# The silu MLP's up products as two pairs of token groups with seven products each: groups 2 and 1 at 512 tokens, groups 3 and 4 as twice 384

## The chip, the cores and the metric

The kernel runs on one core of one Trainium2 chip, as one program. The metric is device time in microseconds (us), median of repeated executions. Beside it there is one profiled execution, read here as rows of its trace: every instruction of the engines TensorE (PE), VectorE (DVE), ScalarE (ACT), GpSimd (POOL) and SyncE (SP), with what each waited for.

## The reference

The inputs are fp32; three layers follow one another:

```python
scores = where(mask, q @ k.T / 8, -1e9)          # 4 batches, 8 heads, 576 positions, head width 64
x = softmax(scores) @ v                          # masks: last 32 positions (heads 0-3), every 32nd (heads 4-7)
x = x.transpose(0, 2, 1, 3).reshape(2304, 512)   # 2304 tokens
x = ((x @ w_a) * (x @ w_b)) @ w_out              # gated MLP, 512 -> 1536 -> 512
h = x @ w_in2                                    # silu MLP, 512 -> 2048
out = (h * sigmoid(h)) @ w_out2                  # 2048 -> 512
```

## The kernel before

**Products.** Every fp32 operand is split into a high and a low part (type fp32r), and each product is three passes: high by high, high by low, low by high (`PASSES`). The 2304 tokens are five groups: 0 to 3 of 512 tokens, group 4 of 256. A hidden piece is 128 hidden units. An "up" product of one piece for one group is 4 blocks of 128 inputs by 3 passes, 12 matmuls whose moving side is as wide as the group: 128x512, or 128x256 for group 4. The down products of the silu MLP have 128 tokens on the output's partitions and 512 outputs as the moving side, so they are 128x512 whatever the group; one hidden piece and 128 tokens are 3 matmuls.

**Direct part.** Up to some 453 us the loop over `PHASES` works through groups 0 and 1 of the gated MLP ("A"), then of the silu MLP ("B"), in blocks of 12 matmuls (`BLOCK`, 2.72 us by the planner). The attention of batches 1 to 3 runs between these products, its units placed by `PLAN` at numbered blocks until `ATT_END`. The weights come packed and are converted there; converted ones are also written to DRAM and read back by the second part.

**Late part.** All after that is a list of events with planned times (`at`, `products`), sorted and issued once (`run_events`); the planner counts 0.2267 us for a 128x512 matmul (`MM`) and 0.12 us for a 128x256 one (`MM_HALF`). It does not measure; on the chip an engine that comes late makes the others wait.

**A pair of groups.** Groups 2 and 3 are taken together: 2x2 blocks of weights by 2x2 blocks of (half of the inputs) by (group) need seven block products in place of eight (Strassen and Winograd). A `Chain` makes these seven for one block of hidden pieces; a `twin` runs two chains in turn, `CHAIN_ORDER` giving the order: 14 steps of 6 matmuls each. After some steps DVE and ACT combine the sums: ACT copies a sum out of PSUM (`u` or `p`), DVE adds the other (L1105), and for the silu MLP ACT takes a tanh (`th`), DVE makes `g` (L1133), ACT casts its high part and DVE subtracts the low part (L806), which gives `h` for the down products of the near group. The far group's `x` rows are kept in SBUF, and its down products run after all twins. DVE and ACT also split the weights (`w`, L1381 and L1380), among them sums of weight blocks `T` (L1390). The near group's down products (L1151, "fillers", 3 matmuls each) are put between the steps by the argument `places`; they are those of the quadrants that this twin and the one before it have finished.

**Order before.** Direct A0, A1, B0, B1; pair (2,3) of the gated MLP, twins then far down (453 to 633 us); group 4's gated MLP (633 to 687); pair (2,3) of the silu MLP, four twins and near down (687 to 805), far down (805 to 849); group 4's silu MLP, 16 pieces up at 128x256 and down (849 to the end).

Of the kernel before, what the change touches and what calls it, by code (L numbers as in the profile page):

```python
# [9 lines left out]
F32 = mybir.dt.float32  # L10
# [7 lines left out]
ALU = mybir.AluOpType  # L18
# [51 lines left out]
PHASES = [("A", 0), ("A", 1), ("B", 0), ("B", 1)]  # L70

HOMES = {"x": (0, 1), "y": (0, 3)}

OPERANDS = ("A11", "A12", "S1", "S2", "S3", "S4", "A22")  # L80
# [9 lines left out]
MM, MM_HALF, BLOCK = 0.2267, 0.12, 2.72  # L90
LEAD_RAW, LEAD_SUM, LEAD_SPLIT = 22.0, 9.0, 6.0

ATT_END = 115
# [8 lines left out]
    2: (37, [41, 49, 58, 66], 78),  # L102
    3: (78, [82, 89, 97, 105], 0),
# [15 lines left out]
def attention_gated_mlp_silu_mlp(  # L119
# [96 lines left out]

    def two(t, n=CC):

        return t.rearrange("p k t -> p (k t)").rearrange("p (s c t) -> p s c t", s=2, c=n)
# [10 lines left out]
    def x_tile(g):  # L230
        if g == NG - 1 and g not in x_t:
            both["s"] = t = home(1)
            x_t[g] = two(t[:, :4])
        if g not in x_t:
            x_t[g] = xpool.tile([P, 2, CC, G], F32R, tag="x%d" % HOMES["x"][g], name="x")
        return x_t[g]
# [482 lines left out]
    def place(c):  # L719
        if c >= STAY:  # L720
            return rpool.tile([P, DM], F32, tag="raw", name="raw")
        if c < CC:
            return pair_home()[:, CC + c]
        if "w" not in both:
            both["w"] = home(3, F32)
        return both["w"][:, c - CC]
# [162 lines left out]
    with tc.manual_schedule():  # L889
# [107 lines left out]
        sp, hs, ops, late = {}, {}, {}, {}  # L997
# [21 lines left out]
        def open_late():  # L1019
            att_ctx.close()  # L1020
            late["pool"] = pool = ctx.enter_context(
                tc.tile_pool(name="late", bufs=1, side="right", reuse_waits="tile")
            )
            t = pool.tile([P, 16, G], F32R, name="operands")
            for m, name in enumerate(("S2", "S1", "A22", "S4")):
                ops[name] = two(t[:, 4 * m:4 * m + 4], 2)
# [4 lines left out]

        def part(name, c, src):
            o = ops[name]
            nc.scalar.copy(out=o[:, 0, c], in_=src())
            nc.vector.tensor_tensor(out=o[:, 1, c], in0=src(), in1=o[:, 0, c].bitcast(F32), op=ALU.subtract)

        def put(key, c, tag, a, b, op):
            sums[key, c] = t = temp(*tag)
            nc.vector.tensor_tensor(out=t, in0=a(), in1=b(), op=op)

        sums = {}

        def operands(r2, r3, t0, step0, t1, step1):

            row = lambda r, c: lambda: r()[:, c]
            got = lambda key, c: lambda: sums[key, c]
            for m, (name, c) in enumerate([(n, c) for n in ("A11", "A12") for c in range(2)]):
                at(t0 + m * step0, part, name, c, row(r2, c + 2 * (name == "A12")))
            work = []
            for c in range(2):  # L1050
                work += [(put, "s1", c, ("p1", c), row(r3, c), row(r3, 2 + c), ALU.add)]
                work += [(put, "s2", c, ("u2", c), got("s1", c), row(r2, c), ALU.subtract)]
                work += [(part, "S2", c, got("s2", c))]
            work += [(part, "S1", c, got("s1", c)) for c in range(2)]
            for c in range(2):
                work += [(put, "s3", c, ("u3", 0), row(r2, c), row(r3, c), ALU.subtract)]
                work += [(part, "S3", c, got("s3", c))]
            work += [(part, "A22", c, row(r3, 2 + c)) for c in range(2)]
            for c in range(2):
                work += [(put, "s4", c, ("u3", 1), row(r2, 2 + c), got("s2", c), ALU.subtract)]  # L1060
                work += [(part, "S4", c, got("s4", c))]
            for m, (f, *a) in enumerate(work):
                at(t1 + m * step1, f, *a)

        def store_row(k):

            n = 2 * (k // 8)
            if n not in late:
                late[n] = home(n or 3, F32)
            return late[n][:, k % 8]  # L1070


        class Chain:
            def __init__(self, n, kind, j, c):
                self.n, self.kind, self.j, self.c = n, kind, j, c
                self.acc, self.q = {}, {}
# [5 lines left out]
            def multiply(self, s):  # L1082
                operand, piece, part, acc, begin = CHAIN[s]
                if begin:
                    self.acc[acc] = ring_tile() if acc == "X" else att_tile(False)
                w, x = sp[self.key(s)], ops[operand]
# [12 lines left out]
            def copied(self, name):  # L1099
                t = temp(name, self.c)  # L1100
# [23 lines left out]
        def gated(chains, quad, row):  # L1124
            out = tpool.tile([P, G], F32, tag="h32", name="h32") if row is None else store_row(row)
# [3 lines left out]
        def silu(chain, quad, row):  # L1129
            th = tpool.tile([P, G], F32, tag="a", name="th")  # L1130
            nc.scalar.activation(out=th, in_=chain.q[quad], func=AF.Tanh, scale=0.5)
            out = tpool.tile([P, G], F32, tag="h32", name="g2") if row is None else store_row(row)
# [11 lines left out]
        def down(accs, w, h, kind, d, first, last):  # L1144

            for wi, xi in PASSES:
                if kind == "o":
                    lhsT, rhs = sp[w][:, wi, d * P:(d + 1) * P], hs[h][:, xi]
                else:
                    lhsT, rhs = hs[h][:, xi, d * P:(d + 1) * P], sp[w][:, wi]  # L1150
                nc.tensor.matmul(  # L1151
                    accs[d], lhsT=lhsT, rhs=rhs, start=(first and wi == 0 and xi == 0), stop=(last and wi == 1)
                )

        def twin(n, kinds, js, half_n, fillers, places):
# [413 lines left out]
```

## Time and profile before

| what | value |
| --- | --- |
| median of 3 runs | 900.23 us (899.98 to 900.32) |
| span of the profiled execution | 897.1 us |
| PE busy | 885.1 us (99%) |
| DVE busy | 621.9 us (69%) |
| ACT busy | 538.0 us (60%) |
| POOL busy | 158.8 us (18%) |

The span runs from the first to the last instruction of the profiled execution. That execution's own time is the span and some 3 us around it, the median of the runs less the span. "Busy" adds up what an engine worked; a queue of matmuls counts as busy while the next waits for nothing.

### The profile page before, as it was taken

The numbers are of one execution on the slowest core, as the hardware profiler recorded it, in microseconds if no ns is written. First come the engines' busy times: TensorE is split into PE (matmuls) and PEld (weight loads), VectorE is DVE, ScalarE is ACT, GpSimd is POOL, SyncE is SP. The second block draws the span as 40 slices with busy tenths as digits, with TensorE's granted clock in tenths as the row PEclk, the third lists the DMA queues.
The fourth block names the chain that finished last, engine by engine and source line by source line (L and its number), as shares of the span: only waits on it lengthen the run. The fifth ranks groups of instructions, "written<-read, shape, count | busy, mean of one in ns | idle before, by whom it ended". The sixth has DMA issues, their size and how long they took to land.

```text
span 897.1 us, 16230 instructions
## 1 busy us (share of the span) xinstructions
PE 885.1 (99%) x5907; PEld 733.4 (82%) x5914; DVE 621.9 (69%) x1123; ACT 538.0 (60%) x1270; POOL 158.8 (18%) x230
## 2 busy tenths in 40 slices
PE   8899999999999999999999999999999999999998
PEld 5578788888888888888888888888999888888897
DVE  4587977758667775767777676765687766775475
ACT  4668898666876765555544434354675555554464
POOL 4545564343432310100000000000000000000000
PEclk9799999999999999999999999999999999999999
DMA  8999899798898982332322212133553221234461
GB/s 175 205 249 294 265 269 311 212 276 247 260 327 259 261 240 95 118 118 94 95 94 71 65 54 71 54 111 99 160 175 110 71 83 51 78 95 164 138 188 40
DMA packets 161584, 142.17 MB, mean 158 GB/s; under 512 B 96656, under 2 KB 119760, under 8 KB 161504
## 3 DMA queue, kind: packets, MB, share of 16 engines
q1 hardware_dynamic: 152166, 117.09, 46.5%
q0 software_dynamic: 7392, 23.23, 7.0%
q10 hardware_dynamic: 1946, 0.81, 0.5%
q8 instruction: 46, 0.75, 0.3%
q14 instruction: 34, 0.28, 0.1%
HBM read 118.55 MB, written 22.54 MB: 157 GB/s over the span
## 4 chain that ended last, share of the span: by engine, by line
PE 88%; DVE 3%; DMA 3%; ACT 2%; SPq 2%; issue 1%; POOL 0%; DVEq 0%; ACTq 0%; POOLq 0%
PE ring L795 24%; PE ring L1090 12%; PE acc L1507 10%; PE att L1090 9%; PE acc L1151 9%; PE acc L1485 6%; PE acc L1277 4%; PE ring L1151 4%; PE att L1151 4%; PE acc L795 3%; DMA words<-in_moe_w_a_dram 1%; PE att L470 1%; PE att L621 1%; PE att L572 1%; SPq L355 1%
## 5 line engine op out<-in xcount | busy, mean ns | idle before, releaser
L795 PE MATMUL ring<-x,w 128*128 128x512 f32 (+1 forms) x816 | 163.0, 354 | 0.4 <-DVE w L788 0.4
L795 PEld LDWEIGHTS ring<-x,w 128*128 128x128 f32 x816 | 133.4, 189 | 21.5 <-DVE w L788 1.0
L1381 DVE TENSOR_TENSOR w<-raw,w 128x512 fp32r<-128x512 f32 (+1 forms) x164 | 106.2, 655 | 28.0 <-ACT w L1380 25.1
L1380 ACT CAST w<-raw 128x512 fp32r<-128x512 f32 (+1 forms) x164 | 95.7, 592 | 19.6 <-PE att L1151 11.0
L795 PE MATMUL ring<-y,w 128*128 128x512 f32 x384 | 93.1, 392 | 0.0
L1507 PE MATMUL acc<-w,h 128*128 128x512 f32 x384 | 92.4, 391 | 0.0
L788 DVE TENSOR_TENSOR w<-raw,w 128x512 fp32r<-128x512 f32 x112 | 83.9, 757 | 9.3 <-ACT w L787 9.0
L1196 POOL DMA_DIRECT2D out_dram<-o x16 | 8.7, 546 | 458.7 <-DVE o L1195 456.2
L1507 PEld LDWEIGHTS acc<-w,h 128*128 128x128 f32 x384 | 71.6, 188 | 15.0
L795 PEld LDWEIGHTS ring<-y,w 128*128 128x128 f32 x384 | 71.5, 188 | 14.9
L805 ACT CAST h<-h 128x512 fp32r<-128x512 f32 (+1 forms) x48 | 27.2, 566 | 77.3 <-DVE h L1126 40.6
L1485 PE MATMUL acc<-h,w 128*128 128x512 f32 x288 | 70.4, 394 | 0.3 <-DVE h L806 0.2
L787 ACT CAST w<-raw 128x512 fp32r<-128x512 f32 x112 | 68.0, 621 | 0.2 <-DVE raw L765 0.2
L1485 PEld LDWEIGHTS acc<-h,w 128*128 128x128 f32 x288 | 53.3, 188 | 12.1 <-DVE h L806 0.5
L806 DVE TENSOR_TENSOR h<-g,h 128x512 fp32r<-128x512 f32 (+1 forms) x64 | 40.5, 632 | 28.9 <-ACT h L805 28.9
L1090 PE MATMUL ring<-operands,w 128*128 128x512 f32 x240 | 58.8, 389 | 0.0
L1090 PE MATMUL att<-operands,w 128*128 128x512 f32 x240 | 58.8, 389 | 0.0
L1090 PE MATMUL ring<-x,w 128*128 128x512 f32 x240 | 58.7, 389 | 0.0
L805 ACT CAST h<-g 128x512 fp32r<-128x512 f32 (+1 forms) x64 | 36.3, 567 | 35.8 <-DVE g L1477 29.1
L740 POOL TENSOR_SCALAR raw<-words 128x512 f16<-128x512 uint8 x56 | 52.1, 931 | 30.9 <-DMA words<-in_moe_w_in_dram 9.9
L1090 PEld LDWEIGHTS att<-operands,w 128*128 128x128 f32 x240 | 45.0, 188 | 9.4
L1090 PEld LDWEIGHTS ring<-operands,w 128*128 128x128 f32 x240 | 45.0, 188 | 9.4
(211 smaller groups left out, 1615.3 us busy)
## 6 DMA issues: line engine op xcount, KB each, us to landing
raw<-keptp SPq DMA_DIRECT2D x80, 256.0 KB
raw<-kepti SPq DMA_DIRECT2D x64, 256.0 KB
words<-in_moe_w_out_dram SPq DMA_DIRECT2D x28, 512.0 KB
raw<-kepto SPq DMA_DIRECT2D x45, 256.0 KB
words<-in_moe_w_in_dram SPq DMA_DIRECT2D x16, 512.0 KB
raw<-keptb SPq DMA_DIRECT2D x32, 256.0 KB
raw<-kepta SPq DMA_DIRECT2D x31, 256.0 KB
words<-in_moe_w_a_dram SPq DMA_DIRECT2D x12, 512.0 KB
```

The costliest lines, as they stand in the source:

```text
L740: nc.gpsimd.tensor_scalar(out=halves_of(made[c], F16, 1), in0=bytes_of(words[c], 8, 7), scalar1=-TINY, scalar2=127.5 * TINY, op0=ALU.mult, ...
L787: nc.scalar.copy(out=o[:, 0], in_=t)
L788: nc.vector.tensor_tensor(out=o[:, 1], in0=t, in1=o[:, 0].bitcast(F32), op=ALU.subtract)
L795: nc.tensor.matmul(ps[:, :T], lhsT=w[:, wi, c * P:(c + 1) * P], rhs=x[:, xi, c, :T], start=(c == 0 and wi == 0 and xi == 0), stop=(c == CC ...
L805: nc.scalar.copy(out=o[:, 0, :T], in_=t32[:, :T])
L806: nc.vector.tensor_tensor(out=o[:, 1, :T], in0=t32[:, :T], in1=o[:, 0, :T].bitcast(F32), op=ALU.subtract)
L1090: nc.tensor.matmul(self.acc[acc], lhsT=w[:, wi, (2 * part + c) * P:(2 * part + c + 1) * P], rhs=x[:, xi, c], start=(begin and c == 0 and m ...
L1151: nc.tensor.matmul(accs[d], lhsT=lhsT, rhs=rhs, start=(first and wi == 0 and xi == 0), stop=(last and wi == 1))
L1380: nc.scalar.copy(out=o[:, 0, cols], in_=t)
L1381: nc.vector.tensor_tensor(out=o[:, 1, cols], in0=t, in1=o[:, 0, cols].bitcast(F32), op=ALU.subtract)
L1485: nc.tensor.matmul(accs[d], lhsT=w[:, wi, d * P:(d + 1) * P], rhs=h[:, xi], start=(j == 0 and wi == 0 and xi == 0), stop=(j == N1 - 1 and ...
L1507: nc.tensor.matmul(accs[t][:, :DM], lhsT=h[:, xi, t * P:(t + 1) * P], rhs=w[:, wi, :], start=(j == 0 and wi == 0 and xi == 0), stop=(j == ...
```

## The change

`PHASES` loses B1. The late part begins with group 4's gated MLP, then takes pair (2,3) of the gated MLP as before. The silu MLP then has two objects `Pair("B", ...)`: groups 2 (near) and 1 (far) at 512 tokens, and groups 3 and 4 together, 768 tokens, as a near and a far half of 384 (`T34`), whose twins' matmuls are 128x384. Their down products stay 128x512, three blocks of 128 tokens for each half. Operand buffers get named slots, and `prepare` sets the operand work's planned times. `ATT_END` and `PLAN` put the attention of batches 2 and 3 into fewer blocks. In the diff's core:

```diff
-PHASES = [("A", 0), ("A", 1), ("B", 0), ("B", 1)]
+PHASES = [("A", 0), ("A", 1), ("B", 0)]
-MM, MM_HALF, BLOCK = 0.2267, 0.12, 2.72
+MM, MM_HALF, MM_SHORT, BLOCK = 0.2267, 0.12, 0.1733, 2.72
-ATT_END = 115
+ATT_END = 103
-    2: (37, [41, 49, 58, 66], 78),
-    3: (78, [82, 89, 97, 105], 0),
+    2: (37, [40, 47, 55, 62], 70),
+    3: (70, [73, 80, 88, 95], 0),
+        class Pair:
+            def __init__(self, mlp, near, far, T, rows):
+                self.mlp, self.near, self.far, self.T, self.rows = mlp, near, far, T, rows
+                self.mm = MM if T == G else MM_SHORT
...
-                    end = products(lambda s=s, chain=chain: chain.multiply(s), 6, MM, [chain.key(s)])
+                    end = products(lambda s=s, chain=chain: chain.multiply(s), 6, pair.mm, [chain.key(s)])
...
+        def fill(pair, g, j, accs):
+            return [fill_one(pair, g, j, d, accs) for d in range(CC if pair.mlp == "A" else pair.T // P)]
...
+        def second(pair, t_near, t_far, last):
+            near, far = {}, {}
+            down_p = lambda f: [x for j in (f, f + 1) for x in fill(pair, pair.near, j, near)]
+            for f in range(0, H2, 2):
+                n = ("p", f, pair.near)
+                if f:
+                    twin(pair, n, "ii", (f, f + 1), H2, down_p(f - 2 + H2) + down_p(f), dict.fromkeys(range(1 + (f == H2 - 2), 15), 1))
+                else:
+                    twin(pair, n, "ii", (f, f + 1), H2, down_p(f), dict.fromkeys(range(9, 15), 1))
+            for filler in down_p(H2 - 2 + H2):
                 products(*filler)
+            results(t_near, near, pair.T // P, nc.gpsimd, "vvvv")
...
+        t_down = second(pair12, groups[2][0], groups[1][0], False)
+        T34 = (groups[4][0] + T4 - groups[3][0]) // 2
+        pair34 = Pair("B", 5, 6, T34, (lambda c: y34()[:, c, :T34], lambda c: y34()[:, c, T34:]))
...
+        second(pair34, groups[3][0], groups[3][0] + T34, True)
```

**Order on TensorE, second to third twin of the pair that it concerns.** Before, in pair (2,3) of the silu MLP: L1090 are the steps of 6 matmuls, L1151 the fillers; the last step of the first chain is the first row, and the last row is the first filler that uses what this step finished.

```order
L1090 MATMUL att<-operands,w 128x512 x6
L1151 MATMUL acc_8085<-w,h 128x512 x3
L1090 MATMUL att<-operands,w 128x512 x6
L1151 MATMUL acc_8108<-w,h 128x512 x3
L1151 MATMUL acc_8124<-w,h 128x512 x3
L1151 MATMUL acc_8137<-w,h 128x512 x3
L1090 MATMUL ring<-x,w 128x512 x6
L1151 MATMUL acc_8085<-w,h 128x512 x3
```

Between the step and that filler stand two steps and four fillers. The same place in the changed kernel, in the pair of halves of 384 tokens (L1129 the steps, L1192 the fillers; `x1a` and `L_8354` are operand slots):

```order
L1129 MATMUL ring<-x3b,w 128x384 x6
L1192 MATMUL acc_8867<-w,h 128x512 x3
L1129 MATMUL ring<-x3b,w 128x384 x6
L1192 MATMUL acc_8884<-w,h 128x512 x3
L1129 MATMUL att<-x1a,w 128x384 x12
L1129 MATMUL ring<-L_8354,w 128x384 x6
L1192 MATMUL acc_8851<-w,h 128x512 x3
```

The two last steps of the twin (`x1a`, x12) now follow each other without a filler, and after the first of them only one step of it and one of the next twin (`L_8354`) stand ahead of the filler that uses its result. A twin there has 12 fillers in place of 16.

**Order on VectorE at the same place.** Before (`u` is the sum that the first chain's last step completes; the two rows of L1133 ahead of it make far rows):

```order
L1133 SCALAR_TENSOR_TENSOR x<-th,ring 128x512 x2
L1381 TENSOR_TENSOR w<-raw,w 128x512 x2
L1105 TENSOR_TENSOR u_8036<-u_8036,att 128x512
L1133 SCALAR_TENSOR_TENSOR g_8156<-th,u_8036 128x512
L806 TENSOR_TENSOR h<-g_8156,h 128x512
```

Behind the far rows there are two weight splits, then the sum. In the changed kernel:

```order
L1174 SCALAR_TENSOR_TENSOR x<-th,ring 128x384
L1416 TENSOR_TENSOR w<-raw,w 128x512 x2
L1174 SCALAR_TENSOR_TENSOR x<-th,ring 128x384
L1425 TENSOR_TENSOR T<-raw 128x256
L1425 TENSOR_TENSOR T<-raw,T 128x256
L1425 TENSOR_TENSOR T<-raw 128x256
L1425 TENSOR_TENSOR T<-raw,T 128x256
L1144 TENSOR_TENSOR u_9040<-u_9040,att 128x384
L1174 SCALAR_TENSOR_TENSOR g_9179<-th,u_9040 128x384
L829 TENSOR_TENSOR h<-g_9179,h 128x384
```

Four sums of weight blocks now stand between the second far row and the sum that leads to `h`.

## Rows read from the trace of the kernel before

**Rows 1.** The page, part 1: busy time of each engine

```profile
PE 885.1 (99%) x5907; PEld 733.4 (82%) x5914; DVE 621.9 (69%) x1123; ACT 538.0 (60%) x1270; POOL 158.8 (18%) x230
```

**Rows 2.** Busy time by stretch; columns as the first line names them

```profile
core 0: us, PE busy (x) PEld busy (x) DVE busy (x) ACT busy (x) POOL busy (x), PEclk, DMA share, GB/s
...
145.00:265.50 120.50, 120.50 (x964) 98.55 (x964) 82.32 (x141) 86.42 (x222) 47.13 (x69) 1.00 0.90 268
265.50:330.00 64.50, 64.50 (x516) 52.78 (x515) 46.59 (x78) 46.04 (x110) 17.64 (x24) 1.00 0.95 272
330.00:453.40 123.40, 123.40 (x784) 101.41 (x783) 85.91 (x149) 68.00 (x167) 8.12 (x11) 1.00 0.32 100
...
687.40:804.60 117.20, 117.20 (x519) 96.80 (x518) 84.97 (x150) 65.43 (x124) 0.00 (x0) 1.00 0.22 70
```

**Rows 3.** PE in time, its longest wait (start, us, work, idle before)

```profile
40.52 2.47 PE L795 MATMUL acc<-x,w 128*128 128x512 f32 x6 [2.62 <-DVE x L654]
```

**Rows 4.** PE in time, two stretches: 128x512 steps, 128x256 blocks

```profile
755.53 1.52 PE L1090 MATMUL ring<-x,w 128*128 128x512 f32 x6
756.89 0.84 PE L1151 MATMUL acc<-w,h 128*128 128x512 f32 x3
...
640.13 3.04 PE L795 MATMUL ring<-x,w 128*128 128x256 f32 x24
643.01 1.60 PE L1277 MATMUL acc<-h,w 128*128 128x256 f32 x12
```

**Rows 5.** Groups by shape from 633 us on (busy us, mean ns | idle before)

```profile
L806 DVE TENSOR_TENSOR h<-g,h 128x512 fp32r<-128x512 f32 x16 | 11.1, 691 | 6.5 <-ACT h L805 6.5
L806 DVE TENSOR_TENSOR h<-g,h 128x256 fp32r<-128x256 f32 x16 | 6.7, 420 | 0.5 <-ACT h L805 0.5
...
L1131 ACT ACTIVATE th<-u 128x512 f32<-128x512 f32 x16 | 10.1, 632 | 19.2 <-DVE u L1105 19.2
L1261 ACT ACTIVATE th<-acc 128x256 f32<-128x256 f32 x16 | 6.2, 385 | 12.1 <-PE acc L795 12.1
```

**Rows 6.** PE from the second twin to the third

```profile
733.10 0.84 PE L1151 MATMUL acc<-w,h 128*128 128x512 f32 x3
...
735.13 0.84 PE L1151 MATMUL acc<-w,h 128*128 128x512 f32 x3
...
740.58 0.84 PE L1151 MATMUL acc<-w,h 128*128 128x512 f32 x3
```

**Rows 7.** DVE in the second twin and on to the third

```profile
727.79 0.69 DVE L1105 TENSOR_TENSOR u<-u,att 128x512 f32<-128x512 f32 x1 [1.86 <-ACT u L1101]
...
733.92 0.69 DVE L1133 SCALAR_TENSOR_TENSOR x<-th,ring 128x512 f32<-128x512 f32 x1 [0.19 <-ACT th L1131]
734.53 1.29 DVE L1381 TENSOR_TENSOR w<-raw,w 128x512 fp32r<-128x512 f32 x2
735.74 0.68 DVE L1105 TENSOR_TENSOR u<-u,att 128x512 f32<-128x512 f32 x1
737.17 0.69 DVE L1133 SCALAR_TENSOR_TENSOR g<-th,u 128x512 f32<-128x512 f32 x1 [0.76 <-ACT th L1131]
738.55 0.69 DVE L806 TENSOR_TENSOR h<-g,h 128x512 fp32r<-128x512 f32 x1 [0.69 <-ACT h L805]
```

**Rows 8.** ACT after the product that ends at 756.89 us

```profile
757.09 0.59 ACT L1101 COPY u<-ring 128x512 f32<-128x512 f32 x1 [2.05 <-PE ring L1090]
```

**Rows 9.** DVE and PE in the second twin: sums T, first activation, first use

```profile
715.90 0.42 DVE L1390 TENSOR_TENSOR T<-raw,T 128x256 f32<-128x256 f32 x1
716.24 0.42 DVE L1390 TENSOR_TENSOR T<-raw 128x256 f32<-128x256 f32 x1
...
722.21 0.69 DVE L806 TENSOR_TENSOR h<-g,h 128x512 fp32r<-128x512 f32 x1
...
722.89 0.84 PE L1151 MATMUL acc<-w,h 128*128 128x512 f32 x3
```

**Rows 10.** The stretch behind PE's longest wait; columns as in rows 2

```profile
41.00:44.40 3.40, 3.40 (x32) 2.39 (x32) 1.10 (x2) 0.54 (x5) 0.78 (x1) 0.50 1.05 173
```

More of the change, by code (lines that the diff above doesn't have):

```diff
@@ L1043, in operands @@
[L1043 to L1063, printed above, removed]
@@ L1170, in twin @@
                         else:
-                            key = (chain.kind, 2, j)
+                            key = (chain.kind, pair.near, j)
                             at(end, keep_act, key, f, *a, None)
@@ L1245, in start4 @@
         def start4(kind, j):
[L1246 to L1247 removed]
+            ps = st4[kind] = ring_tile()
+            up4(kind, j, ps, x_tile(4))
         def copy4():
@@ L1308, in attention_gated_mlp_silu_mlp @@
                 for d in range(CC):
-                    down_one("o", "b", j, d, N1)
-        y3 = lambda: late[0]
-        operands(y2, y3, t_o3 + 6.0, 6.0, t_a4 + 3.0, (clock[0] - t_a4 - 8.0) / 18)
-        accp2 = {}
-        down_p = lambda f: [x for j in (f, f + 1) for x in fill("p", "i", 2, j, j == 0, j == N2 - 1, accp2)]
+                    products(*down_of(j, d))
+        pair = Pair("A", 2, 3, G, (lambda c: x_pair(2)[:, c], lambda c: x_pair(3)[:, c]))
+        pair.prepare(FIRST_OPERANDS, t_open - 22, 4.0)
@@ L1320, in attention_gated_mlp_silu_mlp @@
             else:
-                last_o = [down_of("o", "b", N1 - 1, d, N1) for d in range(CC)]
-                twin(("p", f), "ii", (f, f + 1), H2, last_o + down_p(f), {2: CC, **dict.fromkeys(range(9, 15), 1)})
-        for filler in down_p(H2 - 2 + H2):
+                twin(pair, ("o", f), "ab", (f, f), H1, [down_of(N1 - 1, d) for d in range(CC)], {2: CC})
+        for filler in down_o(H1 - 1):
             products(*filler)
-        results(2, accp2, CC, nc.gpsimd, "vvvv")
-        accp3 = {}
@@ L1341, in attention_gated_mlp_silu_mlp, with save_y, y2 @@
-        down_one("p", "i", N2 - 2, 0, N2)
-        for d in range(T4 // P):
-            for j in ((N2 - 1,), (N2 - 2, N2 - 1))[d]:
-                down_one("p", "i", j, d, N2)
-        for t in range(T4 // P):
-            at(clock[0], lambda t=t: result(groups[4][0], t, acc4["p", t], (epool, tpool)[t], "ea"[t], "va"[t], nc.sync))
+        def save_y(accs, out):
+            for d in range(CC):
+                nc.scalar.copy(out=out()[:, d, :G], in_=accs[d])
+        def y2():
+            if "y2" not in late:
+                late["y2"] = slot("L0", F32)
+            return late["y2"]
@@ new lines, in far_down @@
+        def far_down(pair, act, n, accs, tail=0):
+            for j in range(n):
+                key = (act, pair.far, j)
+                ready[key] = clock[0] - LEAD_SPLIT
+                at(clock[0] - LEAD_SPLIT - 0.1, keep_act, key, pair.row, j)
+                if j < n - tail:
+                    for filler in fill(pair, pair.far, j, accs):
+                        products(*filler)
+        pair12 = Pair("B", 2, 1, G, (lambda c: y2()[:, c], lambda c: ys[1][:, c]))
+        s1 = lambda: tpool.tile([P, G], F32, tag="a", name="s1")
```

284 lines of the change are left out of this document (151 added, 133 removed).

## The prediction

> **What bounds the kernel now.** I read the busy times first: PE works 885.1 of 897.1 us, DVE 621.9, ACT 538.0 [rows 1]. A share over the whole span hides stages, so next the busy time by stretch: in each stretch from 145 to 453 us and in the silu pair's twins (687 to 805 us) PE's busy time is the whole stretch [rows 2]. Then PE's waits in order of length: the longest is 2.62 us at 40.52 us [rows 3], at the start of the kernel, and the late part has none that counts. So the time is the sum of what PE issues, at the pace of its matmuls, and a change is worth the matmuls that it removes, less the waits that it creates where other engines no longer keep up. How near the others are is the last view: in the silu pair's twins DVE is busy 84.97 of 117.20 us [rows 2], but most of its idle time is waiting on ACT inside chains (0.7 us each time, [rows 7]); only one wait per twin, 1.86 us, is real slack [rows 7].
>
> **What the change removes and adds on PE.** Counted in the order of instructions: 128x512 matmuls fall from 3288 to 3096 (192 fewer), 128x256 from 624 to 432 (192 fewer), and 336 of 128x384 come. The silu MLP explains it: one direct group (384 matmuls of 512) becomes the far group of a pair, and 192 up matmuls of 256 for group 4 are merged into seven-product chains of 384. The price of one: six steps of 512 take 756.89 - 755.53 = 1.36 us, 0.2267 each; 24 of 256 take 643.01 - 640.13 = 2.88 us, 0.120 each [rows 4]. A 384-wide one does not occur before. Its bounds are these two, 0.120 and 0.2267; halfway in width, I take halfway in time, 0.1733. The sum: -192 x 0.2267 = -43.5, -192 x 0.120 = -23.0, +336 x 0.1733 = +58.2; together **-8.3 us**. At the two bounds the last term would be 40.3 or 76.2, so the saving could be 26 us or a loss of 10; two points on a line make me give the price 2% either way, 1.2 us.
>
> [...]
>
> **What is moved at no cost.** Group 4's gated MLP goes to the front of the late part, pair (2,3) of the gated MLP behind it: the same matmuls. Pair (2,1) of the silu MLP is pair (2,3)'s pattern with other tokens. The operand splits for the last pair lie in the far down of pair (2,1), 43.5 us of PE; I count some 34 us of DVE there, and without that cover they would cost their own length. The last results leave on SP, and the store behind the last matmul is one block of 128 tokens as before.
>
> **The waits it creates.** They sit in the four twins of the last pair. A step takes 6 x 0.1733 = 1.04 us, a filler 3 x 0.2267 = 0.68. With 12 fillers in place of 16 a twin takes 84 x 0.1733 + 36 x 0.2267 = 22.7 us on PE; one at 512 takes 132 x 0.2267 = 29.9.
>
> *DVE's price.* At 512 an operation of DVE takes 0.691 us, at 256 0.420; of ACT 0.632 and 0.385 [rows 5]. At 384 I take halfway again: 0.555 and 0.51. [...] Issued one behind the other, DVE's operations follow at shorter distances: 0.34 at 256 (715.90 to 716.24, [rows 9]), 0.605 at 512 (two splits, 734.53 to 735.74, [rows 7]), so 0.47 at 384. A twin of the last pair has 38 DVE rows that matter: 10 of 512, 10 of 256, 18 of 384, that is 6.05 + 3.4 + 8.5 = 18 us of issue, and its dozen waits on ACT are some 6 us more (each about 0.5 to 0.6 at 384, against 0.7 at 512). That is 24 us against PE's 22.7: **in these twins DVE is late by about 1.3 us a twin** where it now has 1.9 to spare.
>
> *The chain to an activation.* From the end of the step that completes a sum to the first operation on it: 757.09 - 756.89 = 0.2 us [rows 4, 8]. From the sum to `g` 737.17 - 735.74 = 1.43, from `g` to `h` 1.38, `h` 0.69 [rows 7]. Taking off 0.135 for each DVE operation and 0.12 for each ACT operation gives 1.18 + 1.12 + 0.55 = 2.85 at 384, so 3.05 us with DVE free. Before, PE has 740.58 - 735.13 = 5.45 us between that step and the filler that needs `h` [rows 6], and `h` was done at 739.24 [rows 7].
>
> *Second to third twin.* Now one step of this twin and one of the next stand there: 2 x 1.04 = 2.08 us. Even with DVE free PE waits 3.05 - 2.08 = 1.0. But four sums `T` stand ahead of `u`. Before, the second far row started 733.92 - 733.10 = 0.82 us behind its product [rows 6, 7]; that product now ends 1.72 us (a filler and a step) before our step's end E. So the far row starts at about E - 0.95, and 0.47 and four times 0.34 later `u` may start: E + 0.9. `h` is there at E + 3.7: a wait of 1.65. With DVE 0.8 us late (two thirds of a twin's lag) 2.45. I take **2.5**.
>
> *First to second twin.* A filler, two steps, a filler: 3.44 us, enough for 3.05: 0. *Third to fourth.* Three steps, 3.12 us; DVE free 0, with one us of lag **1.0**. *Behind the fourth.* A step and a filler, 1.72 us: at least 1.35, with lag **1.7**; then the second chain's `h`, 2.85 behind the first against three fillers, 2.04: **0.75**. *First activation of the second twin.* It has no margin at 512 already: `h` ends at 722.90, the filler starts at 722.89 [rows 9]. Now PE passes there with steps a quarter shorter, and the chain shrinks by a fifth only while it carries the same splits of 512: **1.4**. Small ones of the same kind in the other twins: **0.5**. Together **7.9 us**; with DVE free 3.75; with the lag carried over fully from twin to twin some 11.
>
> **The sum.** -8.3 + 7.9 = -0.4 on a span of 897.1, so 896.7; the median of the runs stands 3.1 us above the profiled span. That makes 899.8 us.
>
> **The rivals.** What measurement can tell from no change here is about 0.2%, 1.8 us.
>
> *The waits stay near their floor.* DVE's lag is my estimate from a dozen short terms; if ACT's waits overlap better, or the first activation's chain starts earlier, waits are 3.75 to 6.5 and the time is 895.7 to 898.4. For it: the chains before lose only 0.7 us a time and splits fill gaps between. Against it: the four `T` rows and the fillers that run out are in the order, whatever the lag.
>
> *Slower: the last pair runs at DVE's pace.* Its place is the four twins; it decides when DVE's twin is over 25.3 us, where lag (2.6 a twin, three times, then 2.5 at the end) exceeds 8.3 + 1.8. It gives 11 us of waits and 903. [...]
>
> *Slower: transfers.* The attention from block 37 on gets 66 blocks in place of 78, 180 us in place of 212. Blocks of 2.72 us that end at 453 us put block 37 at 184 and block 115 at 396 us. The DMA share there is 0.90, then 0.95 up to 330 us, then 0.32 [rows 2]: 0.90 x 81 + 0.95 x 64.5 + 0.32 x 66 = 155 us of transfers that must fit into 180. For it: a mean share of 0.86 with peaks near 1 leaves little room. Against it: it fits as a mean, and the idle stretch behind 330 us can take a part. If it binds, PE waits 1 to 5 us: 901 to 905.
>
> *The seven products don't do what the count says.* The counts are in the order, so only the price of 384 columns can fail: each 0.01 us more costs 3.4 us.
>
> **How the numbers follow.** Waits near my 7.9, from 6.3 to 9.7: 0.43, 898.2 to 901.6. Waits nearer to the floor: 0.30, below that. DVE's pace or a clock fall: 0.15. Transfers: 0.09. The price of 384: 0.03, either way. The likeliest gives **899.8 us**. The range reaches from the floor's 895.7 to between the two slower cases' 901 and 905: **895.5 to 903.5**. Faster by over 0.2%, below 898.4: the floor's case and the lower edge of the likeliest, **0.33**. Slower, over 902.0: most of the slower cases, **0.23**. The same: **0.44**.
>
> **What would show it.** Right: 128x384 steps of 1.04 us each; PE waits at DVE's `h` between the second and third twin of the last pair (about 2.5 us, against none now) and behind the fourth, none between the first and second; DVE busy or waiting on ACT through the whole twins; the granted clock at 1.00 there; direct part without waits for loads. Wrong: PE waits for `qld`, `kld` or `words` transfers in the direct part; a lower clock late; steps of 384 not on the line; or waits in pair (2,1), which I hold to be like the pair before.

## The result, and the profile after

The changed kernel takes 910.75 us (909.5 to 911.9, 4 runs) beside 900.11 us of the kernel before on the same chip. The ratio on record is 1.0128, 95% interval 1.0111 to 1.0146 (the two medians alone give 1.0118). It is slower by some 1.2 to 1.3%, where no clear change was forecast. The profiled execution spans 909.8 us, 12.7 more than before, so against the count of matmuls (-8.3) some 21 us were lost. First the page's busy times, as [rows 1] of before:

```profile
PE 889.4 (98%) x5866; PEld 735.2 (81%) x5866; DVE 649.3 (71%) x1193; ACT 549.7 (60%) x1308; POOL 159.2 (17%) x229
```

DVE has 27 us more to do and PE 4 us more, though the matmuls are fewer in columns. Busy time by stretch (columns as in [rows 2]): the direct part's end, group 4's gated MLP, the twins of the last pair, and a short stretch behind its last wait:

```profile
145.00:265.50 120.50, 120.50 (x1002) 98.42 (x1001) 82.23 (x140) 86.18 (x224) 48.28 (x68) 1.00 0.91 261
265.50:330.00 64.50, 60.93 (x525) 47.24 (x524) 45.44 (x77) 45.03 (x112) 20.45 (x28) 1.00 0.84 250
...
374.20:426.60 52.40, 50.69 (x421) 50.45 (x421) 43.85 (x81) 33.08 (x67) 2.20 (x4) 1.00 0.58 182
771.00:872.90 101.90, 96.86 (x482) 86.55 (x482) 75.58 (x149) 58.21 (x124) 1.98 (x4) 0.98 0.28 91
868.20:871.70 3.50, 3.50 (x11) 2.52 (x10) 2.77 (x6) 2.88 (x7) 0.00 (x0) 0.54 0.01 1
```

PE now stands still in three places: 3.6 us between 265 and 330 us, where before it had none, 1.7 us at the start of group 4, 5 us in the last pair; and behind the last of these the granted clock is 0.54 as the mean of 3.5 us, and 0.50 from 868.6 us on. PE's waits by what ended them, from 60 us on:

```profile
PE acc L1192 <- ACT h L828: 4.6, 4, 1.7
PE acc L1547 <- DVE w L811: 1.9, 3, 1.4
PE ring L818 <- DVE h L1269: 1.7, 1, 1.7
PE att L643 <- ACT ptl L603: 0.8, 1, 0.8
```

The first are the last pair's activations, as predicted. The second and fourth lie in the direct part, the third at the start of group 4. (In the rows that follow, a window of the view can cut a group of matmuls short; pace and waits are read from one start to the next.) At the place that the prediction worked out most closely, the second to the third twin, PE's rows (start, us, work) and DVE's read:

```profile
811.16 1.22 PE L1129 MATMUL ring<-x3b,w 128*128 128x384 f32 x6
812.22 0.86 PE L1192 MATMUL acc<-w,h 128*128 128x512 f32 x3
812.92 2.26 PE L1129 MATMUL att<-x1a,w 128*128 128x384 f32 x12
815.02 1.21 PE L1129 MATMUL ring<-L,w 128*128 128x384 f32 x6
817.97 1.33 PE L1192 MATMUL acc<-w,h 128*128 128x512 f32 x3 [1.74 <-ACT h L828]
```

```profile
813.69 0.55 DVE L1174 SCALAR_TENSOR_TENSOR x<-th,ring 128x384 f32<-128x384 f32 x1
814.15 0.42 DVE L1425 TENSOR_TENSOR T<-raw 128x256 f32<-128x256 f32 x1
...
815.28 0.42 DVE L1425 TENSOR_TENSOR T<-raw,T 128x256 f32<-128x256 f32 x1
815.62 0.55 DVE L1144 TENSOR_TENSOR u<-u,att 128x384 f32<-128x384 f32 x1
816.82 0.56 DVE L1174 SCALAR_TENSOR_TENSOR g<-th,u 128x384 f32<-128x384 f32 x1 [0.65 <-ACT th L1172]
817.95 0.56 DVE L829 TENSOR_TENSOR h<-g,h 128x384 fp32r<-128x384 f32 x1 [0.58 <-ACT h L828]
```

The step ends at about 813.96 (half of the x12 row), `u` starts 1.66 us later (0.9 with DVE on time, 1.7 with it late, said the prediction), and the filler that could have run at 816.06 starts at 817.97 with `h`'s high part, its second pass waiting for the low part: 2.28 us in all, where 2.45 was worked out. The pace of 128x384 by itself and between fillers:

```profile
773.17 2.24 PE L1129 MATMUL att<-L,w 128*128 128x384 f32 x12
775.25 1.03 PE L1129 MATMUL ring<-L,w 128*128 128x384 f32 x5
...
781.36 1.22 PE L1129 MATMUL ring<-L,w 128*128 128x384 f32 x6
782.42 0.86 PE L1192 MATMUL acc<-w,h 128*128 128x512 f32 x3
783.12 1.05 PE L1129 MATMUL ring<-x3b,w 128*128 128x384 f32 x5
```

Twelve in a row take 2.08 us from start to start, 0.1733 each, exactly on the line. In turn with 512-wide fillers, six take 1.06 us and three fillers 0.70 in place of 1.04 and 0.68: each change of width cost 0.02 here.

### The profile page after: what moved, and what is told of

It is laid out like the page before. It is cut to its first block, busy times and chain, and to the rows that moved or that the text cites. A ratio compares the mean times of both kernels' runs of the same rounds, so it can differ in the third digit from the quotient of the medians.

```text
span 909.8 us, 16197 instructions
## 1 busy us (share of the span) xinstructions
PE 889.4 (98%) x5866; PEld 735.2 (81%) x5866; DVE 649.3 (71%) x1193; ACT 549.7 (60%) x1308; POOL 159.2 (17%) x229
## 4 chain that ended last, share of the span: by engine, by line
PE 75%; DVE 10%; ACT 6%; DMA 4%; issue 2%; SPq 1%; POOL 0%; ACTq 0%; DVEq 0%; POOLq 0%
PE ring L818 16%; PE ring L1129 14%; PE acc L1192 13%; PE att L1129 10%; PE ring L1192 7%; PE att L1192 5%; PE acc L1519 5%; PE acc L1547 2%; ACT h L828 1%; DVE w L1416 1%; DVE w L811 1%; DMA words<-in_moe_w_a_dram 1%; PE att L492 1%; DMA vl<-in_v_dram 1%; DVE h L829 1%
## 5 line engine op out<-in xcount | busy, mean ns | idle before, releaser
L1129 PE MATMUL ring<-L,w 128*128 128x512 f32 (+1 forms) x504 | 116.5, 374 | 0.0
L1129 PEld LDWEIGHTS ring<-L,w 128*128 128x128 f32 x504 | 93.2, 188 | 15.6
L818 PE MATMUL ring<-x1a,w 128*128 128x256 f32 (+1 forms) x480 | 99.2, 328 | 1.7 <-DVE h L1269 1.7
L1192 PE MATMUL acc<-w,h 128*128 128x512 f32 x336 | 95.1, 400 | 5.0 <-ACT h L828 4.6
L818 PEld LDWEIGHTS ring<-x1a,w 128*128 128x128 f32 x480 | 71.5, 190 | 9.7 <-DVE h L1269 1.9
L1192 PEld LDWEIGHTS acc<-w,h 128*128 128x128 f32 x336 | 62.9, 191 | 18.8 <-ACT h L828 6.0
L1519 PEld LDWEIGHTS acc<-h,w 128*128 128x128 f32 x288 | 53.2, 188 | 12.0 <-DVE h L829 0.5
L1129 PE MATMUL att<-L,w 128*128 128x512 f32 (+1 forms) x240 | 56.2, 379 | 0.0
L1192 PE MATMUL acc<-h,w 128*128 128x256 f32 (+1 forms) x288 | 53.5, 336 | 0.0
L818 PEld LDWEIGHTS ring<-x,w 128*128 128x128 f32 x240 | 44.4, 188 | 10.1 <-DVE w L811 1.0
L1129 PEld LDWEIGHTS att<-L,w 128*128 128x128 f32 x240 | 44.6, 188 | 8.0
L1547 PE MATMUL acc<-w,h 128*128 128x512 f32 x192 | 48.1, 397 | 2.3 <-DVE w L811 1.9
L1192 PEld LDWEIGHTS acc<-h,w 128*128 128x128 f32 x288 | 45.2, 190 | 5.7
```

What stands on the lines that cost most here:

```text
L818: nc.tensor.matmul(ps[:, :T], lhsT=w[:, wi, c * P:(c + 1) * P], rhs=x[:, xi, c, :T], start=(c == 0 and wi == 0 and xi == 0), stop=(c == CC ...
L1129: nc.tensor.matmul(self.acc[acc], lhsT=w[:, wi, (2 * part + c) * P:(2 * part + c + 1) * P], rhs=x[:, xi, c], start=(begin and c == 0 and m ...
L1192: nc.tensor.matmul(o, lhsT=lhsT, rhs=rhs, start=(first and wi == 0 and xi == 0), stop=(last and wi == 1))
L1519: nc.tensor.matmul(accs[d], lhsT=w[:, wi, d * P:(d + 1) * P], rhs=h[:, xi], start=(j == 0 and wi == 0 and xi == 0), stop=(j == N1 - 1 and ...
L1547: nc.tensor.matmul(accs[t][:, :DM], lhsT=h[:, xi, t * P:(t + 1) * P], rhs=w[:, wi, :], start=(j == 0 and wi == 0 and xi == 0), stop=(j == ...
```

## The experiments

All times are ratios to the kernel before on the same chip, with 95% intervals. To read the direct part apart from the start (up to that place executions differ by 3.4 us), I take its length from one and the same matmul, the 104th 128x512 one of fp32 operands (70.83 us before, 71.94 after), to the first matmul behind the direct part (453.42, 374.26). The bf16 matmuls that keep PE busy at the start are not counted, since the two traces hold 41 and 48 of them. In the kernel before this is 382.59, less 384 matmuls of the stage that left, 87.05: 295.54 us. In the changed kernel it is 302.33: **6.8 us more**. Where a wait is given without its row, it is counted from start to start against the pace of the matmuls, which adds 0.1 to 0.2 us to what a row shows, or more where a second pass waits again.

**The plan alone, in the kernel before.**

```diff
-    2: (37, [41, 49, 58, 66], 78),
-    3: (78, [82, 89, 97, 105], 0),
+    2: (37, [40, 47, 55, 62], 70),
+    3: (70, [73, 80, 88, 95], 0),
```

> The kernel before with one edit, the attention's blocks of the change (batches 2 and 3 in blocks 37 to 103 in place of 37 to 115); everything else, the fourth direct stage too, as before. Theory 1 (what the changed kernel loses in its direct part, some 8 us between 265 and 374 us of its trace, comes of the attention in fewer blocks): slower by 5 to 8 us, waits of PE for weight splits (w) and for attention between 265 and 335 us. Rival (the loss comes of the new late part that follows, its loads, its operand work and its buffers): within 1.5 us of before, no waits there.

1.0079 (1.0061 to 1.0097); its direct part, which keeps the fourth stage, is 388.57 us beside 382.59, 6.0 more than before. PE's waits between 260 and 345 us, where the kernel before has none:

```profile
PE acc L1507 <- DVE w L788: 2.0, 3, 1.4
PE att L621 <- ACT ptl L581: 0.7, 1, 0.7
PE acc L1507 <- ACT w L787: 0.4, 1, 0.4
PE att L470 <- DVE x L654: 0.3, 1, 0.3
```

They are the changed kernel's waits, nearly to the tenth. So 6.0 of the direct part's 6.8 us are the attention in 66 blocks in place of 78, whatever follows.

**Wider loads for q and k, fewer products held up, the start of group 4.** Three edits to the changed kernel, each by itself:

```diff
+                        if self.b >= 2:
...
+                            feed[0].dma_start(
+                                out=t[p0:p0 + 32].rearrange("r c j i -> r (c j i)"),
+                                in_=flat[at0:at0 + n].rearrange("(r x) -> r x", r=32),
+                            )
```

> The changed kernel, but the q and k of batches 2 and 3 are loaded from the same tensors in rows of 4608 bytes in place of 128: the same transfers in number and bytes, the same tiles and instructions after them, other values (the attention of these batches is not the reference's). Theory 1a (transfers are the limit where the attention is crowded: ACT stood still 2.8 us for a weight transfer at 264 to 267 us, and the waits of PE follow): the direct part is 5 to 8 us shorter, the time 903 to 906 us. Rival 1b (ACT and DVE are the limit, each in its order, with softmax rows ahead of the activations): DMA share falls, but the direct part stays within 2 us of the changed kernel's, 909 to 912 us.

1.0113 (1.0088 to 1.0139). ACT's wait for a weight transfer, which I had read as the start of it, went; in the changed kernel:

```profile
267.12 0.81 ACT L779 ACTIVATE raw<-words 128x512 uint16<-128x512 uint8 x1 [2.76 <-DMA words<-in_moe_w_out_dram]
```

The same row here, and PE's waits between 260 and 345 us behind it:

```profile
263.38 0.80 ACT L789 ACTIVATE raw<-words 128x512 uint16<-128x512 uint8 x1 [0.21 <-DMA words<-in_moe_w_out_dram]
```

```profile
PE acc L1557 <- DVE w L821: 1.8, 2, 1.4
PE att L653 <- ACT ptl L613: 0.8, 1, 0.8
PE acc L1557 <- ACT w L820: 0.4, 1, 0.4
```

PE's waits stayed: 3.3 us by these rows and a smaller one, beside 3.7 in the changed kernel. Most of this stage's waits are not made by transfers.

```diff
-                    twin(pair, n, "ii", (f, f + 1), H2, down_p(f - 2 + H2) + down_p(f), dict.fromkeys(range(1 + (f == H2 - 2), 15), 1))
+                    twin(pair, n, "ii", (f, f + 1), H2, down_p(f - 2 + H2) + down_p(f), dict.fromkeys(range((3 + 2 * (f == H2 - 2)) if last else 1 + (f == H2 - 2), 15), 1))
```

> The changed kernel with one edit in the last pair (two halves of 384 tokens): the near group's down products start two steps later in each twin from the second on, in the last twin four steps later, so that some are left behind the last step. The same matmuls. Theory 2 (the four waits of 1.55, 2.28, 0.9 and 2.07 us come of too few products between a finished step and the first that needs its activation, and the last of them brings the clock down for 1.8 us): all but some 1 us goes, 7 to 8 us faster than the changed kernel, 903 us. Rival (DVE is the bound of these twins, its work is longer than PE's): the waits move to other places, at most 3 us faster, 908 us or more.

1.012 (1.0102 to 1.0138): the rival's number. The waits for `h` are gone, and others stand in their place, PE's steps waiting for sums that ACT and DVE have not yet taken out of PSUM:

```profile
PE ring L1129 <- ACT p L1140: 3.1, 3, 1.8
PE att L1129 <- DVE u L1144: 1.3, 2, 0.7
```

The later fillers gave DVE no more time in the twin; they only let PE's steps run into DVE's backlog.

```diff
-        pair.prepare(" ".join((S_OPERANDS[0], S1_OPERANDS, S_OPERANDS[1], A22_OPERANDS, LAST_OPERANDS)), t_open + 0.1, 2.6)
+        pair.prepare(" ".join((S_OPERANDS[0], S1_OPERANDS, S_OPERANDS[1], A22_OPERANDS, LAST_OPERANDS)), t_open + 6.1, 2.3)
...
-                result(t0, t, accs[t], pool, tag, "v", nc.gpsimd)
+                result(t0, t, accs[t], pool, tag, "vava"[t], nc.gpsimd)
```

> The changed kernel with two edits at the start of group 4's gated MLP: two of the four results of the direct silu MLP are scaled by ACT in place of DVE, and the operand sums of the pair behind it start 6 us later. Theory 3 (PE's wait of 1.9 us at 378 us is DVE's four results and a sum ahead of the first gate): 1.5 to 2 us faster than the changed kernel. Rival (something else is late there, the weights or the last attention rows): within 0.5 us.

1.0102 (1.0075 to 1.0129), an interval that overlaps the changed kernel's; but the wait at the start of group 4 is gone from the trace. DVE's four results of the stage before and the operand sums behind them were what stood ahead of the first gate (at 379.97 us in the changed kernel):

```profile
375.77 2.48 DVE L1240 TENSOR_SCALAR o<-acc 128x512 f32<-128x512 f32 x4
```

The two edits were made together, so their shares are not told apart.

**Less work on ACT, other orders, in the direct part.**

```diff
+            if self.b >= 2:
+                nc.gpsimd.memset(su, 1.0)
+                ng = segs // 2
+                for i in range(2):
...
+                    nc.scalar.activation(
+                        out=o, in_=x, func=AF.Exp, bias=st["nm"][:, i:i + 1], scale=1.0, accum_out=su[:, i:i + 1]
+                    )
+                return
```

> The changed kernel, but the softmax of batches 2 and 3 takes two exponentials a unit on ACT in place of 4 to 8, without the row sums (this part of the attention is not the reference's; the sums are set to 1 on POOL); all else as it was. Theory 1b (in the direct silu stage, PE waits because the tanh stands behind the exponentials in ACT's order, and DVE's weight splits stand behind the rows that need the tanh): the five waits between 280 and 330 us, 4.4 us, fall below 1.5, and the direct part is 4 to 8 us shorter: 1.004 to 1.008 of the kernel before. Rival (DVE's own masks, maxima and transposes are the load): the waits stay, within 0.2% of the changed kernel's 1.0128.

1.0082 (1.0058 to 1.0105), the direct part 299.63 us, 2.7 less. The waits between 280 and 330 us are 3.5 us in place of 4.4, where the theory had below 1.5 and the rival no change. So ACT's exponentials are a part of it, not the whole.

```diff
+                if step == "X" and p >= NA * 2 and blocks[p][1] == "i":
+                    continue
...
                         acts[j] = split_act(g2, T)
+                        background(p, "softmax")
```

> The changed kernel with one edit: in the blocks of the direct silu stage that make an up product, the exponentials are issued behind that block's activation in place of ahead of it; the same work. Theory 1b: the wait of 1.5 us at 291 us and those at 290 and 324 us go, 3 to 6 us faster, 1.006 to 1.009. Rival (the sum of ACT's and DVE's work in these blocks is the limit, not its order): the waits move, within 0.2% of 1.0128.

1.0124 (1.01 to 1.0149): the rival's number. The waits moved (1.3 us at 315 and at 323 us), their sum stayed.

```diff
-    3: (70, [73, 80, 88, 95], 0),
+    3: (70, [76, 84, 90, 95], 0),
```

> The changed kernel with one edit: the first two of batch 3's four steps of attention start 3 and 4 blocks later, the third 2 (blocks 76, 84, 90, 95 in place of 73, 80, 88, 95). Theory 1c (the direct part loses 6.5 us in steps because attention, weight conversion and the first blocks of the silu stage fall on the same blocks): the steps at 285 to 291 us shrink by 2 us or more, some of it coming back behind block 90; 1.008 to 1.011. Rival (the loss goes with the mean density alone): the sum of the steps stays within 1 us of 6.5.

1.0255 (1.0237 to 1.0272). The first waits shrank, to 0.4 and 0.9 us, but the tighter steps behind them made waits of 1.5 and 1.7 us at 325 and 330 us and of 3.5 and 3.6 at 335 and 358 us, and behind each of the last two the granted clock fell to 0.50 (from 340.6 us for 3.4 us, from 361.1 us for 6.8 us); as the mean of an execution it is 0.985 to 0.989 in all four runs, beside 0.989 to 0.998 in the changed kernel's. This tells of placing, and is far dearer than either theory said.

```diff
-CONV_B = (34, 1.8)
+CONV_B = (33, 1.6)
```

> The changed kernel with one edit: the silu MLP's weights are converted one piece every 1.6 blocks from block 33, in place of 1.8 from 34, so that conversion ends at block 82 in place of 89. Theory 1c: the steps at 313 to 330 us (blocks 88 to 94 or so) lose the conversion beside them and shrink by 1 us or more, those at 285 to 291 us grow or stay. Rival (conversion has no part in it): the steps stay as they are, within 0.2% of 1.0128.

1.0098 (1.0083 to 1.0113), the direct part 299.78 us, 2.6 less. Between 260 and 345 us there are left:

```profile
PE acc L1547 <- DVE w L811: 1.4, 1, 1.4
PE acc L1547 <- ACT w L810: 0.4, 1, 0.4
```

The waits at 313 to 330 us are gone with the conversion beside them. So what is lost there hangs on ACT's and DVE's work on three things at once: attention, conversion of weights, and the chain of the silu stage.

**DVE in the last pair.** Two ways to take the weight sums from it. On POOL, and planned 5 us earlier (the edits also took the sums of the gated pair's sixth twin along):

```diff
-                nc.vector.tensor_tensor(out=o, in0=i, in1=j, op=ALU.subtract)
+                (nc.gpsimd if n[-1] == 5 else nc.vector).tensor_tensor(out=o, in0=i, in1=j, op=ALU.subtract)
...
-                ts = t - LEAD_SUM + LEAD_SPLIT
+                ts = t - LEAD_SUM + LEAD_SPLIT - 5.0 * (n[-1] == 5)
```

> The changed kernel with the weight sums (T) of the last pair on POOL in place of DVE, planned 5 us earlier; the same values. The last experiment showed that holding products back only moves the waits to the buffers that DVE and ACT empty late. Theory 2b (DVE is the bound of the last pair's twins, by 8 sums of 0.34 us in each): the waits of 6.8 us in the twins and the clock's fall behind them go down to 3 to 4 us together, the latency that is left with DVE free; 4 to 5 us faster, 1.007 to 1.009. Rival (the chain ACT-DVE-ACT-DVE to an activation is the whole of it): the waits stay within 1.5 us, 1.011 to 1.0128.

1.0098 (1.0075 to 1.012): waits of 4.0 us stay, 1.4 of them new (the first twin's sums). With products held back and the start of group 4 mended as well:

> The changed kernel with three edits together: the weight sums of the last pair on POOL, its down products held back as in the earlier experiment, and the two edits at the start of group 4's gated MLP that took its wait away. Theory 2b with a free DVE both causes are gone: waits in the last pair under 1.5 us, no clock fall there, 9 us faster than the changed kernel, 1.002 to 1.004 of the kernel before. Rival (ACT is the next bound in these twins): waits for ACT's copies of 3 us and more stay, 1.006 or more.

1.0066 (1.0043 to 1.0089): 4.6 us of waits were left, so the rival's number. The reason is in two rows of that run's DVE beside POOL's:

```profile
797.40 0.74 POOL L1425 TENSOR_TENSOR T<-raw 128x256 f32<-128x256 f32 x1 [20.01 <-DVE w L1416]
798.22 1.07 POOL L1425 TENSOR_TENSOR T<-raw,T 128x256 f32<-128x256 f32 x1
...
797.52 1.17 DVE L1416 TENSOR_TENSOR w<-raw,w 128x512 fp32r<-128x512 f32 x1 [0.20 <-ACT w L1415]
798.61 1.09 DVE L829 TENSOR_TENSOR h<-g,h 128x384 fp32r<-128x384 f32 x1
```

A split of 0.69 us takes 1.17 while POOL works, an `h` of 0.56 takes 1.09. DVE paid back what it saved: from the first to the last 384-wide matmul it is busy for 69.8 us here and in the changed kernel alike. So the sums, which both silu pairs need alike, were kept in DRAM by pair (2,1) instead, and read back (also planned 5 us earlier):

```diff
+            if n[0] == "p" and n[2] == 5:
+                nc.sync.dma_start(out=t, in_=summed_kept[n[1], c])
+                return
...
+            if n[0] == "p":
+                summed_kept[n[1], c] = d = dpool.tile([P, 2 * DM], F32, tag="keptT%d%d" % (n[1], c), name="keptT")
+                nc.sync.dma_start(out=d, in_=t)
```

> The changed kernel with one edit: the weight sums (T), which both silu pairs need alike, are written to DRAM by the pair (2,1) and read back by the last pair in place of being added again; the same values. DVE loses 8 rows of 0.34 us in each twin of the last pair, and no POOL work takes their place (with the sums on POOL, DVE's splits of 0.69 us took 1.1 to 1.2 while POOL worked). Theory 2b (DVE is late in these twins): its waits fall from 6.8 us to some 4, the latency with DVE free, less of the clock's fall: 3 to 5 us faster, 1.008 to 1.0095. Rival (the chain's latency is the whole of it): waits within 1 us of before, 1.011 to 1.0128.

1.0054 (1.0039 to 1.0069), 0.7% faster than the changed kernel by this alone. Waits in the last pair:

```profile
PE acc L1192 <- ACT h L828: 1.3, 2, 1.0
```

From start to start, without the last `h`, they are 2.4 us where 4 were expected: DVE's lag was more of the waits than my floor had left it.

> The edit of the kept weight sums, with the last pair's down products held back, and with the start of group 4's gated MLP as in the earlier experiment that took its wait away. Theory 2b: with DVE free and the products held back, less than 1.5 us of waits is left in the last pair, and no fall of the clock: 9 to 10 us faster than the changed kernel, 1.001 to 1.003 of the kernel before; what is left is the direct part. Rival (ACT's copies out of PSUM are the next bound): 3 us of waits stay, 1.005 or more.

1.0016 (1.0006 to 1.0026), one wait of 0.7 us left in the last pair, for ACT's copy out of PSUM. With DVE free, holding back works.

**The direct part again.** On this kernel, conversion every 1.4 and every 1.25 blocks, and 1.4 with a later first step:

> The best kernel so far (kept weight sums, products held back, start of group 4 mended; 1.0016 of the kernel before) with one more edit: the silu MLP's weights are converted one piece every 1.4 blocks from block 33, ending at block 76. Theory 1c (the direct part's 6.5 us are the attention in fewer blocks beside conversion and the silu stage; ending at 82 took 2 us of them away): the steps at 313 to 330 us are gone and most of the 2.5 us at 285 to 291 too, 3 to 5 us faster, 0.996 to 0.999 of the kernel before. Rival (the steps at 285 to 291 us are attention and the three first silu blocks alone): only the 2 us, 0.999 to 1.0005.

0.9997 (0.9987 to 1.0007). The wait of 1.5 us at 288 us and those from 314 us on went, others came at 264 to 294 us, one of 2.4; the direct part is 301.92 us, as much as with 1.8 blocks (301.85). The number is the rival's, but its reason, that only the waits at 285 to 291 us stay, is not what the trace shows.

> The same with one piece every 1.25 blocks, so that conversion ends at block 71, before the direct silu stage begins at 72. Theory 1c: no waits from 270 to 330 us, unless the denser conversion makes new ones between 190 and 265 us: 5 to 6 us faster than 1.0016, 0.995 to 0.997. Rival (transfers: 512 KB of words every 3.4 us beside the attention's loads are too dense): waits for words or raw weights between 190 and 265 us, 1.000 or more.

1.0013 (1.0001 to 1.0024): the rival's number. PE's own waits, from 251 us on, end on splits and activations, but the engines that convert now wait for transfers between 190 and 265 us. ACT's waits for packed weights there, of which the kernel with 1.8 blocks has none:

```profile
ACT raw L779 <- DMA words<-in_moe_w_out_dram: 1.8, 1, 1.8
ACT raw L779 <- DMA words<-in_moe_w_in_dram: 1.7, 1, 1.7
```

POOL waits 7.5 us for them, beside 2.4 with 1.8 blocks. So transfers are a likely limit to converting earlier.

> As with 1.4 blocks a piece, and batch 3's first two steps of attention two blocks later (75, 82, 88, 95), behind the first three up products of the silu stage. Theory 1c: the step at 285 to 291 us goes as well, 0.995 to 0.997. Rival (the tighter steps behind it make waits of their own, as those of 84, 90, 95 did): 0.999 or more.

1.0065 (1.0049 to 1.0081): the rival, a wait of 3.3 us for attention from 330 us on, with a fall of the clock for 6.8 us; the mean granted clock of this execution, 0.986, is the lowest of all profiled ones here.

> The kernel with kept weight sums, products held back and the start of group 4 mended (1.0016 of the kernel before), with one more edit: conversion every 1.6 blocks from block 33. In the changed kernel this rate took 2 us of the direct part's loss away; 1.4 and 1.25 moved or added to it. If the loss is a matter of how the work of ACT and DVE falls on the blocks: 2 us faster, 0.999 to 1.0005. If it is a constant sum that only moves: 1.001 to 1.002.

**0.9973 (0.9962 to 0.9983): 896.26 us beside 898.97, faster than both kernels**, and faster than either side had put it. From 60 us on PE's two longest waits are:

```profile
PE acc L1553 <- DVE w L811: 1.4, 1, 1.4
PE ring L1129 <- ACT p L1140: 0.6, 1, 0.6
```

Its direct part is 298.54 us, 3.3 less than with 1.8 blocks.

> The same, and the softmax of batches 2 and 3 with two exponentials a unit in place of 4 to 8 and without the row sums (that part of the attention is not the reference's). If ACT's and DVE's work beside the direct silu stage is what the loss is made of, less of it takes another 2 to 3 us: 0.995 to 0.998 of the kernel before, which is what the count of products promised. If the loss is something else, as without it: 0.999 to 1.0005.

0.9956 (0.9944 to 0.9968), direct part 296.79 us: 1.7 less again with fewer exponentials, as the theory had it.

## Why the prediction was wrong

**Right.** The count and its price: 0.1733 a matmul, -8.3 us. That the waits of the last pair eat it: 7.9 us forecast, 7.1 measured (counted from start to start against the pace; the rows of waits show less, since a wait for `h`'s low part lies inside a group). Place by place: none against 0 from the first to the second twin, 2.28 against 2.5, 0.90 against 1.0, 2.07 against 1.7 behind the fourth, 1.55 against 1.4 at the second twin's first activation, 0.3 against 0.5 for small ones. The row of the place behind the fourth:

```profile
866.70 6.35 PE L1192 MATMUL acc<-w,h 128*128 128x512 f32 x18 [1.53 <-ACT h L828]
```

The forecast's wait of 0.75 for the last `h` (0.81 by its own terms, 2.85 - 2.04) does not show by itself: the clock's fall stretches PE's work there. In the fourth experiment's execution, where the clock fell at 817 us instead, 0.6 us of it are there. That DVE sets the pace in these twins was shown by the kept sums (waits down to 2.4 us), and by holding back alone, which only moved the waits.

**The step that failed** is "what is moved at no cost", and with it "direct part without waits". I costed the attention in fewer blocks by its transfers alone and gave it a chance of 0.09; the direct part cost 6.8 us. The place was that rival's, and the plan alone gave 6.0 of it in the kernel before; its cause was not. Wider transfers took ACT's wait for a transfer away and left PE's waits; fewer exponentials and another rate of conversion changed them. What I left out is that the fourth direct stage was cover: attention could run into the stretch from 330 to 453 us, where ACT worked 68.00 of 123.40 us [rows 2]. Without the stage attention's work on ACT and DVE falls on blocks where they also convert weights and serve the silu chain. Neither is full there (45 of 64.5 us each between 265 and 330 us, and by total busy time no more than before [rows 2]); they are late because each keeps its order and waits for the other. For the longest wait the rows show it, PE's, ACT's and DVE's in turn:

```profile
281.60 2.88 PE L818 MATMUL ring<-y,w 128*128 128x512 f32 x12
...
293.03 2.56 PE L1547 MATMUL acc<-w,h 128*128 128x512 f32 x10 [1.38 <-DVE w L811]
```

```profile
284.02 0.35 ACT L533 ACTIVATE prs<-sm,nm 128x64 f32<-128x64 f32 x1 [1.09 <-DVE nm L518]
...
288.40 0.57 ACT L1509 ACTIVATE th<-ring 128x512 f32<-128x512 f32 x1
```

```profile
289.00 0.69 DVE L1511 SCALAR_TENSOR_TENSOR g<-th,ring 128x512 f32<-128x512 f32 x1 [1.97 <-ACT th L1509]
...
291.88 2.12 DVE L811 TENSOR_TENSOR w<-raw,w 128x512 fp32r<-128x512 f32 x2
```

The up product is done by about 284.5 us. ACT's tanh of it comes at 288.40, behind eight exponentials (from 284.02 us on) and the cast and conversion of weights; DVE stands still 1.97 us for it, and its weight splits, which PE waits for, come behind. For the other waits this reading is not shown row by row, and a changed order on ACT alone only moved them. Of the 6.8 us, the runs tie 6.0 to the plan; 0.8 are not taken apart.

**Mis-sized or missed terms.** The start of group 4 was to have no stall: 1.9 us, DVE's four results and operand sums, removed by the fourth experiment. Changes of width: some 84 in the twins by 0.02, 1.7 us, which no row before could show. The clock's fall, to which the forecast gave 0.15 together with DVE's pace, I had sized at 1.7 us, an estimate from the 3.4 us at 0.50 in [rows 10]; no row of the kernel before shows a fall in the late part. In this execution one came behind the last wait and cost 1.6 us. Behind the wait between the second and third twin the clock stayed at 1.00 (817.97 to 821.5 us); in the fourth experiment's execution it fell there, to 0.73 as the mean of 815.4 to 818.9 us. The sum: -8.3 + 6.8 + 1.9 + 7.1 + 1.6 + 1.7 = 10.8. The spans differ by 12.7, of which 1.1 lie in the start, ahead of the matmul from which the direct part is counted; so 0.8 is not accounted for. The 3.1 us that the forecast set between span and median are no fixed piece either: in every run here an execution's own time is 1.7 to 1.9 us above its span, and the rest was a difference between executions.

**The best version** (conversion every 1.6 blocks) keeps -8.3, pays 3.0 in the direct part, 1.7 for width and 0.8 in the last pair: -2.8 by this sum, -2.7 measured between the medians.

## What to carry to other kernels

When a stage is taken out, ask what ran in its shade: the work that loses its cover must be counted on every engine, not only on the queue that looked full. Where two engines wait for each other in fixed orders, don't take a busy share for slack: ACT and DVE were each busy for 45 of 64.5 us here, and PE waited for them; look for the place where the spare time was. Where DVE was late, moving consumers back alone only moved the wait (1.012 beside 1.0128); work had to leave the engine, and here to memory (1.0054) rather than to POOL (1.0098), beside which DVE's split took 1.17 us in place of 0.69.

## What the runs showed of the hardware

**The clock fell behind some of PE's waits, in some executions.** Behind PE's wait of 1.53 us that ends at 866.70 us it was 0.54 for 3.5 us (above). Behind the wait of 1.38 us that ends at 293.03 us it stayed at 1.00 in the changed kernel; behind the same wait in the changed kernel with conversion every 1.6 blocks it fell:

```profile
291.00:295.00 4.00, 2.62 (x11) 1.84 (x12) 3.56 (x7) 2.42 (x5) 3.31 (x4) 1.00 0.86 193
```

```profile
288.90:292.30 3.40, 3.32 (x8) 2.65 (x9) 2.72 (x5) 1.24 (x3) 3.18 (x5) 0.53 1.02 253
```

The length of the wait alone doesn't tell: in the changed kernel the clock stayed at 1.00 behind the 1.74 us that end at 817.97 us, and with conversion every 1.4 blocks behind a wait of 2.19 us. In the last pair, where PE is dense, the fall cost about 1.6 us: eight matmuls of the fillers (starts from 868.60 to 871.58 us) take 0.427 us each in place of 0.227. In the direct part less of it shows: the fourth experiment, which changes nothing there, has a fall at 291 us (0.59 as the mean of 4 us), and its direct part is 0.4 us longer than the changed kernel's. The changed kernel's two runs with a mean granted clock of 0.989 and 0.990 took 911.6 and 911.9 us, the two with 0.994 and 0.998 took 909.9 and 909.5: falls are likely one reason for such differences.

**POOL's sums and DVE slowed each other.** In the run with POOL's sums and products held back a split goes from 0.69 to 1.17 us and an `h` from 0.56 to 1.09 while POOL adds tiles of SBUF (797.40 to 805.04 us), and both have 0.69 and 0.56 again behind it; POOL's own rows go from 0.74 to 1.18. DVE's sums `u` and `p`, with one input in PSUM, keep their 0.55 us in that run.
